# The first 26 MLP steps of a three-stage kernel, and all scan and weight work beside them, as static pinned lists

## The chip, the cores and the metric

One core of a Trainium2 chip runs the whole program. It has five engines with an instruction queue each, which run in order and wait for each other by semaphores: TensorE (PE, matmuls; PEld is its weight load), VectorE (DVE), ScalarE (ACT), GpSimd (POOL) and SyncE (SP, which issues most transfers here). The metric is the device time of one execution in microseconds. A kernel's time is the median of several runs; beside these stands one profiled execution, whose trace the rows below come from.

## The reference

A gated linear attention, an MLP with a silu gate and a top-1 mixture of eight experts, one after the other, all in 32-bit floats:

```python
f = 1.0 / (1.0 + np.exp(-f_logit))              # q, k, v, f_logit: (4, 8, 768, 48)
for t in range(S):
    state = f[:, :, t, :, None] * state + np.einsum('bhd,bhe->bhde', k[:, :, t], v[:, :, t])
    y[:, :, t] = np.einsum('bhd,bhde->bhe', q[:, :, t], state)
x = y.transpose(0, 2, 1, 3).reshape(3072, 384)
h = x @ w_in                                     # (384, 2048)
x = (h * (1.0 / (1.0 + np.exp(-h)))) @ w_out     # (2048, 384)
...
expert_idx = np.argmax(x @ w_gate, axis=1)       # 8 experts, 384 -> 1024 -> 384, relu
```

## The kernel before

The 3072 tokens are 24 chunks of 128 (six to a batch entry). A chunk n of the scan goes through these pieces of work: its gate logits f_n are clamped on DVE, go through exp and ln on ACT, and are summed along time by a matmul with a triangular matrix (pl_n); ACT makes en_n and ep_n of that; DVE multiplies them into k and q (kpad, qpad); PE transposes both (pk_n, pq_n), ACT copies them out (kt_n, qt_n); PE makes the scores (sc_n, two banks), DVE masks them (am_n); PE makes the outputs from the state, from the masked scores, and the gain of the state (py_n and pyb_n); ACT copies y_n, DVE carries the state, PE flips y_n (pt_n), and ACT and DVE make the high and low half of x from it (big for chunks 0 and 1, xth and xtl of group g after that). Chunks 0, 1 form group 0, chunks 2, 3 group 1, chunks 4 to 6 group 2, whose f is one tile, called f_4.

The MLP works on one group g and one sixteenth i of the 2048 hidden columns at a time; that pair is a step. `moe_h` makes ph_g_i (nine matmuls: high and low halves of x and w_in), then se (tanh, ACT) and sg (DVE); `moe_g` splits sg into gh (ACT) and gl (DVE); `moe_o`, two steps later, multiplies them by a piece of w_out into px (six matmuls for two chunks, nine for three). Steps 0 to 5 belong to group 0, steps 6 to 11 to group 1, and from step 12 on both take turns, hidden piece by hidden piece. In the same time 16 pieces each of w_in and w_out arrive, with 64 bits to a number; DVE converts a piece in three instructions (in_cv, out_cv), ACT takes the high half (in_hi, out_hi) and DVE the low one (in_lo, out_lo).

A long written list, `OPENING`, sets the order of everything ahead of step 0; its instructions are pinned, which means that they stay on their engine in the order in which they were written. Behind it a plan gives each piece of work a step (`ST0` to `ST6`, `UI`, `UO`, `LD`), and the loop over the steps writes a step's ph, its planned work, its split and its px. On PE that order is kept; on DVE, ACT and SP a scheduler orders the unpinned instructions at build time, by its own estimate of when they are ready. The PSUM banks of the tag a are three, and all of a chunk's pl, pk, pq, sc, py, pyb and pt take them in turn; a new tile waits until the readers of the tile before it in its bank are done.

Of the kernel before, what the change touches and what calls it, by code (L numbers as in the profile page):

```python
# [43 lines left out]
FILL = {2: 4}  # L44
# [3 lines left out]
ST0 = (-15, -12, -10, -8, -6, -4)  # L48
ST1 = (-12, -11, -7, -5, -3, -1)
ST2 = (-9, 0, 0, 1, 3, 4)  # L50
ST3 = (-1, 2, 3, 4, 5, 5)
ST4 = (-2, 3, 5, 7, 9, 11)
ST5 = (7, 10, 12, 16, 16, 18)
ST6 = (14, 17, 20, 22, 24, 26)
LAST = ((5, 4), (3, 5))
F_HOME = {2: 'lfh', 3: 'lfl'}
LD = (-30, -30, -10, -1, 0, 5, 11)
S1 = (-2, 1, 3, 5, 6, 8)
ASH = 3
# [7 lines left out]
UI = (-9, -9, -9, 0, 1, 1, 3, 5, 6, 8, 9, 11, 13, 15, 17, 19)  # L67
UO = (-9, -9, -9, 1, 2, 3, 5, 6, 8, 10, 11, 13, 15, 17, 19, 21)
# [4 lines left out]
GACT = 9  # L73
# [4 lines left out]
LOV = (0, 0)  # L78
# [7 lines left out]
ST = ST0, ST1, ST2, ST3, ST4, ST5, ST6  # L86
# [11 lines left out]
def kernel(  # L98
# [71 lines left out]
    BANKS = {0: "haahhaaa", 1: "haahhaaa"}  # L170
# [84 lines left out]
    def load_piece(kind, i):
        u, h = divmod(i, 4)
        src = moe_w_in if kind == "in" else moe_w_out
        nm = f"{kind}_{i}"
        if h == 0:
            new_unit((kind, u))  # L260
        shape = [P, KC, P] if kind == "in" else [P, 1, DM]
        if src.dtype == I64:
            t = raw.tile(shape + [2], U32, tag="raw", name=f"{nm}_raw")
            made = len(pieces_made)
            pieces_made.append(i)
            load_raw(t.rearrange("p c f w -> p c (f w)"), src, kind, i, nc.scalar if made < 0 else nc.sync)
            x = raw.tile([P, ROW], U32, tag="cv", name=f"{nm}_cv", bufs=2)[:, :DM].rearrange("p (c f) -> p c f", c=shape[1])
            t2 = t.rearrange("p c f w -> p (c f) w")
            narrow(t2, x.rearrange("p c f -> p (c f)"), i < (PI if kind == "in" else PO))
            x = x.bitcast(F32)  # L270
        else:
            x = raw.tile(shape, F32, tag="raw", name=f"{nm}_raw")
            nc.sync.dma_start(out=x, in_=part_of(src, kind, i, 1))
        split((kind, u), h, x if kind == "in" else x[:, 0], nc.vector)
# [58 lines left out]
    pieces_made = []  # L333
# [43 lines left out]
    def narrow(r, x, pin=False):  # L377
        for k in range(3):
            if pin and k == 0:
                strict.append(1)  # L380
            narrow_op(r, x, k, ve)
            if pin and k == 0:
                strict.pop()
# [9 lines left out]
    def clamp(t, pin=lambda fn: fn):  # L393
        pin(nc.vector.tensor_scalar_max)(t, t, FMIN)

    def log1(t, pin=lambda fn: fn):
        pin(nc.scalar.activation)(t, t, AF.Ln, bias=1.0)

    def att0(n):
        f = loaded.pop(("f", n))  # L400
        g, _ = group_of[n]
        if g < 2 or n == starts[g]:
            t = f if g < 2 else fb[g][:, : sizes[g]]
            pin = keep if g == 2 else lambda fn: fn
            if g != 2:
                clamp(t)
            pin(nc.scalar.activation)(t, t, AF.Exp, scale=-1.0)
            if g != 2:
                log1(t)
# [6 lines left out]
        (nc.scalar.copy if n < EARLY else nc.vector.tensor_copy)(hi, f2)  # L416
        nc.vector.tensor_sub(lo, f2, hi.bitcast(F32))
# [155 lines left out]
    def att4(n):  # L573
# [4 lines left out]
        warm(y_banks(n)[0], FILL.get(n, 0))  # L578
# [101 lines left out]
    def moe_h(g, i):  # L680
# [13 lines left out]
        (keep(nc.scalar.activation) if (g, i) == (0, 0) else nc.scalar.activation)(e, ph[:, :GT], AF.Tanh, scale=0.5)  # L694
        t = att.tile([P, GT], F32, tag="sg", name=f"sg_{g}_{i}", bufs=SG)
        nc.vector.scalar_tensor_tensor(out=t, in0=e, scalar=1.0, in1=ph[:, :GT], op0=ALU.add, op1=ALU.mult)  # L696
        ht[g, i] = t

    def moe_g(g, i):
# [4 lines left out]
        (nc.scalar.copy if g < GACT else nc.vector.tensor_copy)(hi, t)  # L704
        (nc.gpsimd if (g, i) < LOV else nc.vector).tensor_sub(lo, t, hi.bitcast(F32))  # L705
# [642 lines left out]
    for n in range(NCH):  # L1348
        g, r = group_of[n]
        if n < len(ST):  # L1350
            so = ST[n]
            s0 = ld = LD[n]
        else:
            s0 = pos[g, 0] - NF + r * NF // sizes[g] - ASH
            so = [s0 + x for x in S1]
            s0 = ld = s0 - 4
        if n == 2:
            at(so[1], spread_ends, 2, sy)
            at(so[1], lambda: (open_high("out", 2), open_low("out", 2)))
        for j, st in enumerate(stages):  # L1360
            if n > 1 and (n, j) not in OPENED:
                (at_end if (n, j) in LAST else at)(so[j], st, n)
        if g < 2:
            if n == 3:
                at(ld, load_chunk, n, "kq")
        else:
            if r == 0:
                for m in range(n, n + sizes[g]):
                    if g > 2:
                        at(s0, load_chunk, m, "f")  # L1370
            at(ld, load_chunk, n, "qk")
        if n > 2:
            at(ld + 1, load_chunk, n, "v")
    for i in range(16):
        for nm, slots in (("in", UI), ("out", UO)):
            if (nm, i) not in OPEN_PIECES:
# [184 lines left out]
```

## Time and profile before

| | |
|---|---|
| median of the runs (lowest to highest, 3 runs) | 837.82 us (836.27 to 840.59) |
| profiled execution: time, span | 833.39 us, 831.7 us |
| PE busy | 802.9 us, 97% of the span |
| DVE busy | 469.1 us, 56% |
| ACT busy | 377.4 us, 45% |
| POOL busy | 65.2 us, 8% |
| mean granted PE clock | 0.992 of full speed |
| transfers | 99.10 MB, mean 119 GB/s |

The span runs from the first instruction to the last. PE's busy time counts a matmul from start to modelled end, so it says when PE had work, not that the work went at full speed. Matmuls, and also the instructions of DVE and ACT, overlap a little with their followers; the cost of one in a dense stretch is read from start to start. Where an engine sat idle, the views name what ended the wait.

### The profile page before, as it was taken

What the parts mean: (1) busy time and instruction counts of PE and PEld (TensorE: products, weight loads), DVE (VectorE), ACT (ScalarE), POOL (GpSimd) and SP (SyncE); (2) the same over time, 40 slices, a digit from 0 to 9 for tenths busy, and PEclk for the clock granted to TensorE, in tenths of its full rate; (3) what the DMA queues carried; (4) which work ended last, traced back from release to release, by engine and by line L of the source; (5) the groups of instructions that cost most, each with busy time, mean ns of one, the idle gap of its engine ahead of it and who ended that gap; (6) DMA issues with size and microseconds to landing.
All of it is one profiled execution on the core that took longest, in us unless ns stands there. A gap on an engine that the chain in (4) does not pass through costs nothing.

```text
span 831.7 us, 15598 instructions
## 1 busy us (share of the span) xinstructions
PE 802.9 (97%) x5840; PEld 754.2 (91%) x5840; DVE 469.1 (56%) x1258; ACT 377.4 (45%) x836; POOL 65.2 (8%) x111
## 2 busy tenths in 40 slices
PE   8789989999999999999999999999999999999994
PEld 5679889989999999999999999999899999989994
DVE  7889964555555556646655646466574426245520
ACT  5644454453453454435445333355473426455520
POOL 2000100001000100100100000101200010111001
PEclk9999899999999999999999999999999999999998
DMA  9855546222443343342433321423281617645500
GB/s 215 205 153 159 182 127 202 65 51 67 110 93 86 96 105 79 105 104 65 119 81 77 95 82 40 134 58 125 90 291 44 206 39 265 221 145 169 170 16 28
DMA packets 171813, 99.10 MB, mean 119 GB/s; under 512 B 115756, under 2 KB 165341, under 8 KB 171728
## 3 DMA queue, kind: packets, MB, share of 16 engines
q1 hardware_dynamic: 167342, 87.34, 38.1%
q0 software_dynamic: 3280, 9.49, 3.1%
q10 hardware_dynamic: 1106, 1.18, 0.4%
q8 instruction: 48, 0.79, 0.4%
q14 instruction: 37, 0.30, 0.1%
HBM read 78.76 MB, written 16.33 MB: 114 GB/s over the span
## 4 chain that ended last, share of the span: by engine, by line
PE 77%; DVE 8%; issue 7%; DMA 3%; ACT 2%; POOL 1%; SPq 0%; POOLq 0%; ACTq 0%; DVEq 0%
PE ph L423 22%; PE px L423 22%; PE po L423 7%; PE p L423 7%; PE pya L423 3%; PE sc L423 3%; PE pyb L423 2%; PE pl L423 1%; PE pk L428 1%; PE plt L428 1%; DMA w_raw<-in_moe_w_dram 1%; POOL out_dram L1002 1%; PE p_r L423 1%; PE pq L428 1%; PE po_r L423 1%
## 5 line engine op out<-in xcount | busy, mean ns | idle before, releaser
L423 PE MATMUL px<-out_lo,gh 128*128 128x384 f32 x384 | 137.0, 357 | 0.3 <-ACT gh L704 0.3
L696 DVE SCALAR_TENSOR_TENSOR sg<-se,ph 128x384 f32<-128x384 f32 (+1 forms) x144 | 72.9, 507 | 113.1 <-ACT se L694 110.3
L694 ACT ACTIVATE se<-ph 128x384 f32<-128x384 f32 (+1 forms) x143 | 64.9, 454 | 150.2 <-PE ph L423 142.1
L423 PE MATMUL px<-out_hi,gl 128*128 128x384 f32 x384 | 129.5, 337 | 0.0
L423 PE MATMUL px<-out_hi,gh 128*128 128x384 f32 x384 | 128.8, 335 | 0.0
L423 PE MATMUL ph<-xth,in_lo 128*128 128x384 f32 (+1 forms) x384 | 124.3, 324 | 1.5 <-ACT xth L657 1.2
L423 PE MATMUL ph<-xtl,in_hi 128*128 128x384 f32 (+1 forms) x384 | 122.8, 326 | 2.5 <-DVE sg L696 1.9
L423 PE MATMUL ph<-xth,in_hi 128*128 128x384 f32 (+1 forms) x384 | 124.0, 323 | 0.0
L704 ACT CAST gh<-sg 128x384 fp32r<-128x384 f32 (+1 forms) x144 | 68.9, 478 | 63.3 <-DVE sg L696 60.6
L705 DVE TENSOR_TENSOR gl<-sg,gh 128x384 fp32r<-128x384 f32 (+1 forms) x144 | 73.5, 510 | 32.1 <-ACT gh L704 31.2
L423 PEld LDWEIGHTS ph<-xtl,in_hi 128*128 128x128 f32 x384 | 72.1, 189 | 4.3 <-DVE sg L696 2.6
L423 PEld LDWEIGHTS px<-out_lo,gh 128*128 128x128 f32 x384 | 72.3, 188 | 3.8 <-issue 1.1
L423 PEld LDWEIGHTS ph<-xth,in_lo 128*128 128x128 f32 x384 | 72.6, 189 | 2.4 <-ACT xth L657 1.4
L423 PEld LDWEIGHTS px<-out_hi,gl 128*128 128x128 f32 x384 | 72.3, 188 | 0.8 <-DVE gl L705 0.3
L423 PEld LDWEIGHTS ph<-xth,in_hi 128*128 128x128 f32 x384 | 72.6, 189 | 0.0
L423 PEld LDWEIGHTS px<-out_hi,gh 128*128 128x128 f32 x384 | 72.1, 188 | 0.0
L423 PE MATMUL po<-w_lo,hh 128*128 128x384 f32 (+4 forms) x184 | 62.9, 342 | 0.0
L423 PE MATMUL po<-w_hi,hl 128*128 128x384 f32 (+4 forms) x184 | 62.0, 337 | 0.0
L423 PE MATMUL po<-w_hi,hh 128*128 128x384 f32 (+4 forms) x184 | 61.9, 336 | 0.0
L253 DVE TENSOR_TENSOR w_lo<-w_raw,w_hi 128x384 fp32r<-128x384 f32 x104 | 52.5, 551 | 13.0 <-ACT w_hi L252 12.9
L423 PE MATMUL p<-xsl,w_hi 128*128 128x480 f32 (+6 forms) x168 | 58.4, 347 | 0.0
L423 PE MATMUL p<-xsh,w_hi 128*128 128x480 f32 (+6 forms) x168 | 58.3, 347 | 0.0
(290 smaller groups left out, 1465.4 us busy)
## 6 DMA issues: line engine op xcount, KB each, us to landing
w_raw<-in_moe_w_dram SPq DMA_DIRECT2D x64, 384.0 KB
xs<-big SPq DMA_DIRECT2D x8, 776.0 KB
in_again<-in_moe_w_in_dram SPq DMA_DIRECT2D x16, 384.0 KB
out_again<-in_moe_w_out_dram SPq DMA_DIRECT2D x16, 384.0 KB
in_raw<-in_moe_w_in_dram SPq DMA_DIRECT2D x15, 384.0 KB
xe<-xs SPq DMA_DIRECT2D x7, 776.0 KB
out_raw<-in_moe_w_out_dram SPq DMA_DIRECT2D x14, 384.0 KB
f<-in_f_logit_dram SPq DMA_DIRECT2D x24, 192.0 KB
```

Source lines behind the costliest of these rows:

```text
L253: (keep(lo_engine.tensor_sub) if pin else lo_engine.tensor_sub)(lo[:, h], x, hi[:, h].bitcast(F32))
L423: ins = nc.tensor.matmul(*a, **k)
L428: ins = nc.tensor.transpose(*a, **k)
L694: (keep(nc.scalar.activation) if (g, i) == (0, 0) else nc.scalar.activation)(e, ph[:, :GT], AF.Tanh, scale=0.5)
L696: nc.vector.scalar_tensor_tensor(out=t, in0=e, scalar=1.0, in1=ph[:, :GT], op0=ALU.add, op1=ALU.mult)
L704: (nc.scalar.copy if g < GACT else nc.vector.tensor_copy)(hi, t)
L705: (nc.gpsimd if (g, i) < LOV else nc.vector).tensor_sub(lo, t, hi.bitcast(F32))
L1002: ins = nc.gpsimd.indirect_dma_start(out=out[:, :], out_offset=bass.IndirectOffsetOnAxis(ap=idx[:n], axis=0), in_=o[:n], in_offset=None, b ...
```

## The change

Everything up to step 26 is now written out. `OPENING` ends a little differently, and a new list `STEPS` gives for each of the steps 0 to 26 three strings: what is written ahead of its ph, between ph and split, and behind its px. In these strings ci0:6 is the first conversion instruction of w_in piece 6, hi and Li its high and low half, co, ho, Lo the same for w_out, li and lo the loads; the other names are those of the scan's pieces of work. All of it is pinned, ph's tanh, sg, gh and gl too. A step converts one piece: two instructions ahead of ph, the third behind sg; the high and low half of a piece are made one step after its conversion. The gate logits of chunks 4 to 6 move from the opening to steps 1 to 4, with a table load on each side of their ln; those of chunks 7 to 9 are fixed in steps 17 to 21. The table that has tanh is loaded by hand behind ln of f_3. Chunk 1's sum takes another bank, the four warm-up matmuls ahead of chunk 2's outputs are dropped, and chunk 5 (the last of its batch entry) no longer writes its decay for the state.

```diff
-OPENING = '... kmul:1 qmul:1 ends:1 f:2 li:2 a:1 f:3 F:4 F:5 F:6 k:2 q:2 lo:2 sc:0 ...'
+OPENING = '... kmul:1 qmul:1 ends:1 f:2 f:3 li:2 a:1 k:2 q:2 li:3 sc:0 ... exp:2 log:2 exp:3 log:3 table:0 ...'
+STEPS = (
+    ('ci0:3 ci1:3', 'ci2:3 lo:3 fk:2 fq:2 kt:2 qt:2', ''),
...
+    ('co0:3 co1:3', 'co2:3 lo:6 hi:5 Li:5 st:2 fk:3 fq:3 kt:3 qt:3 a:3 fclamp:2 fexp:2', 'pt:2 xh:2 xl:2'),
...
-FILL = {2: 4}
...
-ST2 = (-9, 0, 0, 1, 3, 4)
-ST3 = (-1, 2, 3, 4, 5, 5)
-ST4 = (-2, 3, 5, 7, 9, 11)
...
-UI = (-9, -9, -9, 0, 1, 1, 3, 5, 6, 8, 9, 11, 13, 15, 17, 19)
-UO = (-9, -9, -9, 1, 2, 3, 5, 6, 8, 10, 11, 13, 15, 17, 19, 21)
...
-    BANKS = {0: "haahhaaa", 1: "haahhaaa"}
+    BANKS = {0: "haahhaaa", 1: "xaahhaaa"}
...
-        warm(y_banks(n)[0], FILL.get(n, 0))
...
-        (keep(nc.scalar.activation) if (g, i) == (0, 0) else nc.scalar.activation)(e, ph[:, :GT], AF.Tanh, scale=0.5)
+        ac.activation(e, ph[:, :GT], AF.Tanh, scale=0.5)
...
-        nc.vector.scalar_tensor_tensor(out=t, in0=e, scalar=1.0, in1=ph[:, :GT], op0=ALU.add, op1=ALU.mult)
+        ve.scalar_tensor_tensor(out=t, in0=e, scalar=1.0, in1=ph[:, :GT], op0=ALU.add, op1=ALU.mult)
...
+        table=lambda n: ac.preload_act_table_set("exp_and_others"),
...
-    for s in range(first, total):
-        if s >= 0:
-            moe_h(*seq[s])
+    for s in range(total):
+        pre, mid, end = STEPS[s] if s < len(STEPS) else ("", "", "")
+        if s == len(STEPS):
+            strict.clear()
+        steps(pre)
+        moe_h(*seq[s])
+        steps(mid)
         for fn, args in plan.get(s, ()):
             fn(*args)
-        if s >= 0:
-            moe_g(*seq[s])
+        moe_g(*seq[s])
         if s >= LAG:
             moe_o(*seq[s - LAG])
+        steps(end)
```

**Place 1: ACT ahead of step 0's tanh (se_0_0).** Before:

```order
L224 ACTIVATE f_3_237<-f_3_237 128x384 x2
L224 COPY y_1_365<-py_1_325 128x12x16
L224 COPY y_1_365<-pyb_1_326 128x12x16
L224 CAST in_0_hi_144<-in_2_cv_359 128x384
L224 CAST big_92<-pt_1_373 128x384
L224 ACTIVATE en_2_378<-pl_2_368 128x384
L224 ACTIVATE ep_2_380<-pl_2_368 128x384
L224 ACTIVATE f_4_239<-f_4_239 128x1152 x2
L224 ACT_TABLE_LOAD
L224 ACTIVATE se_0_0_415<-ph_0_0_402 128x256
```

and now:

```order
L236 ACTIVATE f_3_233<-f_3_233 128x384 x2
L236 ACT_TABLE_LOAD
L236 CAST big_92<-pt_0_339 128x384
L236 CAST in_0_hi_144<-in_1_cv_314 128x384
L236 COPY y_1_366<-py_1_329 128x12x16
L236 COPY y_1_366<-pyb_1_330 128x12x16
L236 CAST in_0_hi_144<-in_2_cv_363 128x384
L236 CAST big_92<-pt_1_374 128x384
L236 ACTIVATE en_2_379<-pl_2_369 128x384
L236 ACTIVATE ep_2_381<-pl_2_369 128x384
L236 ACTIVATE se_0_0_418<-ph_0_0_405 128x256
```

Both halves of f_3's work and the table load stand ahead of x high of chunk 0 (big from pt_0), and exp and ln of f_4 are gone from ahead of se_0_0.

**Place 2: PE at steps 2 and 3,** where chunk 2's outputs (py_2) and ph_0_3 follow px of step 0. Before:

```order
L423 MATMUL px_0_1_555<-out_0_hi_134,gh_0_0_451 128x384
L423 MATMUL ph_0_3_562<-big_92,in_0_hi_144 128x256
...
L423 MATMUL py_2_576<-ones_80 128x512
...
L423 MATMUL py_2_576<-state_86,qt_2_433 128x48
...
L423 MATMUL py_2_576<-v_2_392,am_2_0_479 128x48
...
L423 MATMUL py_2_576<-v_2_392,kpad0_89 64x48 x8
L428 MATMUL pq_3_611<-ident_77,qpad1_88 112x128 x4
L428 MATMUL pk_3_616<-ident_77,kpad1_90 112x128 x4
```

and now:

```order
L408 MATMUL px_0_1_537<-out_0_hi_134,gh_0_0_439 128x384
L408 MATMUL py_2_544<-state_86,qt_2_437 128x48
...
L408 MATMUL py_2_544<-v_2_297,am_2_0_483 128x48
...
L408 MATMUL py_2_544<-v_2_297,kpad0_89 64x48 x8
L408 MATMUL ph_0_3_578<-big_92,in_0_hi_144 128x256
...
L413 MATMUL pk_3_599<-ident_77,kpad1_90 112x128 x4
L413 MATMUL pq_3_604<-ident_77,qpad1_88 112x128 x4
```

The outputs of chunk 2 stand ahead of ph_0_3, without the matmuls on ones, and k is transposed ahead of q. Chunk 3's outputs move ahead of ph_0_5 in the same way; those of chunks 4 to 6 move by one to three steps, in either direction.

**Place 3: DVE from the carry of chunk 2 to the masks of chunk 3.** Before:

```order
L595 TENSOR_TENSOR state_86<-py_2_576,state_86 112x4x48
L596 TENSOR_TENSOR state_86<-state_86,a_all_85 112x4x48
L452 SCALAR_TENSOR_TENSOR kpad0_89<-en_4_627,k_4_441 128x8x48
L458 TENSOR_TENSOR qpad0_87<-q_4_439,ep_4_629 128x8x48
L224 TENSOR_SCALAR out_5_cv_638<-out_5_raw_636 128x384
L369 SCALAR_TENSOR_TENSOR out_5_cv_638<-out_5_raw_636,out_5_cv_638 128x384
L696 SCALAR_TENSOR_TENSOR sg_0_4_674<-se_0_4_672,ph_0_4_662 128x256
L373 SCALAR_TENSOR_TENSOR out_5_cv_638<-out_5_raw_636,out_5_cv_638 128x384
L661 TENSOR_TENSOR xtl_1_681<-pt_2_676,xth_1_680 128x384
L705 TENSOR_TENSOR gl_0_4_699<-sg_0_4_674,gh_0_4_698 128x256
L523 TENSOR_TENSOR am_3_0_694<-sc_3_0_684,trir_78 128x512
L253 TENSOR_TENSOR out_1_lo_541<-out_5_cv_638,out_1_hi_540 128x384
```

and now:

```order
L236 TENSOR_TENSOR state_86<-py_2_544,state_86 112x4x48
L236 TENSOR_TENSOR state_86<-state_86,a_all_85 112x4x48
L236 TENSOR_SCALAR f_4_491<-f_4_491 128x1152
L236 TENSOR_TENSOR gl_0_3_618<-sg_0_3_590,gh_0_3_617 128x256
L236 TENSOR_TENSOR xtl_1_632<-pt_2_627,xth_1_631 128x384
L236 TENSOR_SCALAR out_4_cv_635<-out_4_raw_463 128x384
L236 SCALAR_TENSOR_TENSOR out_4_cv_635<-out_4_raw_463,out_4_cv_635 128x384
L236 SCALAR_TENSOR_TENSOR sg_0_4_650<-se_0_4_648,ph_0_4_638 128x256
L236 SCALAR_TENSOR_TENSOR out_4_cv_635<-out_4_raw_463,out_4_cv_635 128x384
L236 TENSOR_TENSOR out_0_lo_135<-out_3_cv_575,out_0_hi_134 128x384
L236 TENSOR_TENSOR am_3_0_667<-sc_3_0_657,trir_78 128x512
L236 TENSOR_TENSOR am_3_1_669<-sc_3_1_658,trir_78 128x512
```

The clamp of f_4 stood in the opening and is now here, ahead of gl_0_3; conversions come one piece to a step where they came two pieces side by side. On ACT the same stretch now reads:

```order
L236 COPY kt_3_609<-pk_3_599 112x512
L236 COPY qt_3_611<-pq_3_604 112x512
L236 ACTIVATE f_4_491<-f_4_491 128x1152
L236 CAST gh_0_3_617<-sg_0_3_590 128x256
L236 CAST xth_1_631<-pt_2_627 128x384
L236 ACTIVATE se_0_4_648<-ph_0_4_638 128x256
L236 CAST out_0_hi_134<-out_3_cv_575 128x384
L236 CAST gh_0_4_671<-sg_0_4_650 128x256
L236 ACT_TABLE_LOAD
L236 ACTIVATE f_4_491<-f_4_491 128x1152
L236 ACT_TABLE_LOAD
L236 COPY y_3_709<-py_3_683 128x12x16
```

Here exp of f_4 stands ahead of gh_0_3, and its ln with two table loads ahead of the copy of y_3; before, both stood in the opening (place 1).

## Rows read from the trace of the kernel before

**Rows 1.** Windows view, a row per stretch: its length, busy PE, PEld, DVE, ACT, POOL, PEclk

```profile
24.70:61.50 36.80, 29.08 (x256) 25.14 (x256) 30.42 (x70) 20.02 (x43) 0.00 (x0) 1.00 0.70 185
61.50:92.00 30.50, 30.15 (x248) 28.83 (x248) 28.65 (x71) 15.35 (x39) 0.00 (x0) 1.00 0.52 150
92.00:102.00 10.00, 9.07 (x48) 8.10 (x48) 9.66 (x23) 3.92 (x11) 3.19 (x1) 0.66 0.59 193
102.00:119.00 17.00, 14.72 (x107) 13.24 (x107) 9.58 (x24) 10.95 (x21) 1.87 (x2) 1.00 0.70 190
119.00:142.00 23.00, 23.00 (x177) 22.89 (x178) 12.34 (x30) 9.39 (x25) 0.88 (x5) 1.00 0.45 151
```

**Rows 2.** Waits of PE from 24.7 to 142 us: in total, times, longest

```profile
PE ph L423 <- DVE sg L696: 1.9, 2, 1.5
PE sc L423 <- ACT kt L500: 1.4, 1, 1.4
PE pk L428 <- ACT y L570: 1.4, 1, 1.4
PE ph L423 <- DVE in_lo L253: 1.3, 1, 1.3
...
PE ph L423 <- ACT in_hi L224: 1.1, 1, 1.1
...
PE py L423 <- DVE am L523: 0.7, 1, 0.7
```

**Rows 3.** Windows view around 95 us, columns as in rows 1

```profile
94.00:95.00 1.00, 1.00 (x13) 0.91 (x11) 1.00 (x4) 0.00 (x0) 0.82 (x1) 0.73 0.93 311
95.00:101.00 6.00, 6.00 (x26) 5.71 (x27) 5.75 (x14) 1.94 (x6) 2.37 (x1) 0.50 0.54 174
101.00:102.00 1.00, 1.00 (x5) 0.85 (x4) 0.91 (x3) 1.00 (x4) 0.00 (x0) 0.86 0.94 304
```

**Rows 4.** Timeline of PE: start, us, instruction, count, around chunk 2's outputs

```profile
38.30 1.04 PE L423 MATMUL py<-ones 128*128 128x512 bf16 x4
39.27 0.31 PE L423 MATMUL py<-state,qt 48*128 48x48 f32 x1
...
42.81 0.65 PE L428 MATMUL pq<-ident,qpad 128*112 128x128 f32 x4
```

**Rows 5.** Timeline of DVE near 90 us: start, us, instruction

```profile
89.21 0.41 DVE L696 SCALAR_TENSOR_TENSOR sg<-se,ph 128x256 f32<-128x256 f32 x1
89.54 0.35 DVE L365 TENSOR_SCALAR out_cv<-out_raw 128x384 uint32<-128x384 uint32 x1
89.81 0.55 DVE L369 SCALAR_TENSOR_TENSOR in_cv<-in_raw,in_cv 128x384 uint32<-128x384 uint32 x1
90.28 0.55 DVE L369 SCALAR_TENSOR_TENSOR out_cv<-out_raw,out_cv 128x384 uint32<-128x384 uint32 x1
...
92.36 1.28 DVE L523 TENSOR_TENSOR am<-sc,trir 128x512 f32<-128x512 f32 x2
93.55 0.54 DVE L253 TENSOR_TENSOR in_lo<-in_cv,in_hi 128x384 fp32r<-128x384 f32 x1
```

**Rows 6.** Timeline of ACT ahead of step 0's tanh

```profile
25.28 2.38 ACT L224 ACTIVATE f<-f 128x1152 f32<-128x1152 f32 x2
27.67 1.28 ACT L224 ACT_TABLE_LOAD   x1
28.96 0.38 ACT L224 ACTIVATE se<-ph 128x256 f32<-128x256 f32 x1
```

**Rows 7.** Timeline of DVE: the one conversion that waited for its piece

```profile
103.37 0.36 DVE L365 TENSOR_SCALAR in_cv<-in_raw 128x384 uint32<-128x384 uint32 x1 [0.85 <-DMA in_raw<-in_moe_w_in_dram]
```

**Rows 8.** Chain that ended last: start, us, groups of matmuls

```profile
46.38 1.05 PE px L423 x6
47.42 1.06 PE ph L423 x9
48.81 1.09 PE sc L423 x16
```

More of the change, by code (lines that the diff above doesn't have):

```diff
@@ L77 @@
 PD = 2
-LOV = (0, 0)
 VS = 44
@@ L250, in split @@
         pin = key[0] in ("w1", "w2") and key[1] == 0 or key[:2] == ("w1", 1)
-        pin_hi = pin or (key, h) == (("in", 0), 3)
-        (keep(nc.scalar.copy) if pin_hi else nc.scalar.copy)(hi[:, h], x)
+        (keep(nc.scalar.copy) if pin else nc.scalar.copy)(hi[:, h], x)
         (keep(lo_engine.tensor_sub) if pin else lo_engine.tensor_sub)(lo[:, h], x, hi[:, h].bitcast(F32))
[L255 to L274, printed above, removed]
     opened = {}
@@ L375, in narrow_op, with narrow @@
             )
-    def narrow(r, x, pin=False):
+    def narrow(r, x):
         for k in range(3):
[L379 to L383, printed above, removed]
+            narrow_op(r, x, k, nc.vector)
     lf = {}
@@ L401, in att0 @@
         g, _ = group_of[n]
[L402 to L409, printed above, removed]
+        if g > 3 and n == starts[g]:
+            for k in range(3):
+                f_group(g, k)
         if n < PLAIN:
@@ L1047, in rest_fetch @@
         w = nt * P
-        r = [raw.tile([P, ROW], F32, tag="cv", name=f"xe_r_{t}", bufs=2) for t in range(nt)]
+        r = [raw.tile([P, ROW], F32, tag="cv", name=f"xe_r_{t}", bufs=CVB) for t in range(nt)]
         for t in range(nt):
@@ L1349 @@
         g, r = group_of[n]
[L1350 to L1359, printed above, removed]
-        for j, st in enumerate(stages):
[L1361 to L1376, printed above, removed]
-                at(slots[i], load_piece, nm, i)
+        if n < LISTED:
+            continue
+        s0 = pos[g, 0] - NF + r * NF // sizes[g] - ASH
+        for j, st in enumerate(stages):
+            at(s0 + S1[j], st, n)
+        s0 -= 4
+        if g > 3 and r == 0:
+            for m in range(n, n + sizes[g]):
+                at(s0, load_chunk, m, "f")
+        at(s0, load_chunk, n, "qk")
+        at(s0 + 1, load_chunk, n, "v")
     for j in range(2 * NF):
@@ new lines, with steps @@
+    for nm, kind in (("i", "in"), ("o", "out")):
+        do["l" + nm] = lambda i, kind=kind: open_load(kind, i, queue((kind, i) in FIRST))
+        do["h" + nm] = lambda i, kind=kind: open_high(kind, i)
+        do["L" + nm] = lambda i, kind=kind: open_low(kind, i)
+        do["c" + nm] = lambda i, kind=kind: [open_join(kind, i, k) for k in range(3)]
+        for part in range(3):
+            do[f"c{nm}{part}"] = lambda i, kind=kind, part=part: open_join(kind, i, part)
+    def steps(text):
+        for step in text.split():
```

105 lines of the change are left out of this document (39 added, 66 removed), and 25 rows, old and new, of the table STEPS.

## The prediction

> **What bounds the kernel now.** I first took the windows view, to see in which stretch TensorE (PE) leaves time unused [rows 1]. From 119 us on, PE is busy without a gap, and the pages of the stretches behind show the same dense picture; what can be won lies between 24.7 us, where MLP step 0 starts, and 119 us. The reader is to take the length less the PE busy time of each row: 36.80 - 29.08 = 7.72, 30.50 - 30.15 = 0.35, 10.00 - 9.07 = 0.93 and 17.00 - 14.72 = 2.28, together 11.28 us idle.
>
> The waits of PE say what those gaps are [rows 2]: single waits, most of them 1.1 to 1.5 us long, each for another engine's result: the gated product sg on VectorE (DVE), the transposed keys on ScalarE (ACT), the y copy that frees a PSUM bank, the low and the high half of a weight piece, the masks. None is a long lack of data; they are results that an in-order engine made too late because other work stood ahead of them. In the first window DVE is busy for 30.42 of 36.80 us, in the second for 28.65 of 30.50: DVE is nearly full while it converts the weight pieces, and it works far ahead: after 119 us it is busy for only 12.34 of 23.00.
>
> The windows around 95 us show a second loss [rows 3]: the granted clock goes from 1.00 to 0.50 (1.2 in place of 2.4 GHz) for about seven microseconds. Lost are 0.27 + 6 x 0.50 + 0.14 = 3.41 us of PE at full clock. Just before, chunk 5's 48-column products had waited for their masks (am, 0.7 in [rows 2]).
>
> Last, the four warm-up matmuls ahead of chunk 2's output take from 38.30 to 39.27 us [rows 4]: 0.97 us of PE on nothing. **The most the change can give** is thus 11.28 + 3.41 + 0.97 = 15.7 us.
>
> **The change, part by part.** It leaves the amount of work as it is (but for the four warm-ups, two more table loads and three small transfers for chunk 5, whose state nobody reads) and fixes who stands behind whom on every engine up to step 26. I cost it by what still waits afterwards.
>
> The DVE load first. Start to start, DVE takes 0.33 for sg, 0.27 for the first conversion instruction, 0.47 for each of the other two and for a low half, 1.19 for a pair of masks [rows 5]. A piece is 0.27 + 3 x 0.47 = 1.68, a step with its sg and gl 1.68 + 2 x 0.33 = 2.34. A PE step is one ph and one px: 1.06 + 1.05 = 2.11 [rows 8]. So in steps without attention work DVE is the slower by 0.23; the attention matmuls turn it round: a chunk costs PE some 6 us (two transpose groups of 0.65 and outputs from 39.27 to 42.81, 3.54 [rows 4], scores 1.09 [rows 8]) and DVE an estimated 3.2, by the nearest forms of [rows 5] (k and q products and x low like a low half, 3 x 0.47, masks 1.19, two narrow state operations 0.6). Over 26 steps and nearly five chunks PE has 26 x 2.11 + 4.9 x 6 = 84 us and DVE 27 x 1.68 + 26 x 0.66 + 4.9 x 3.2 = 78, plus 2 for clamps and splits of f. PE stays the longer one, and before sg each new step has two conversion instructions that fill the time in which DVE would wait for ph and its tanh. A PE step needs gl of two steps earlier, so a lag of some 4 us on DVE costs nothing. I cost the steady part of the list at nothing; the cover is that lag. If it went, each of some 14 steps without much attention would lose 0.23, 3.2 us.
>
> *Step 0.* Before, ACT has behind ep of chunk 2 the exp and ln of chunks 4 to 6 (2.38) and a table load (1.28), and only then tanh of step 0, at 28.96 [rows 6]. These 3.66 us leave this place. In exchange exp and ln of f_3 and the table load now stand ahead of x high of chunk 0: 1.28 and an estimated 0.8 (a third of the 2.38, for a third of the columns), while before ACT had to wait there for the flip of y; DVE gives some of it back, because the clamp of f_4 to f_6 (an estimated 0.7, three times the columns of an instruction of 0.27) has left the opening. I expect step 0 to start within 0.5 us of before and the scores of chunk 2 about 1.6 us earlier. The waits for kt (1.4), for the weight halves of piece 3 (1.1 and 1.3) and for the y copy (1.4) go, since piece 3 is converted in step 0 and needed in step 3, and chunk 2's outputs stand a step earlier. Left here: about 0.4 for q's product and 0.6 for the masks of chunk 2, together 1.0.
>
> *Step 4, where a new wait comes.* The clamp of f_4 now stands on DVE behind the state of chunk 2; behind it stands gl_0_3, which needs gh_0_3, and gh_0_3 stands on ACT behind exp of f_4, which needs the clamp. So DVE waits for exp (1.19, half of the pair in [rows 6]) and gh (0.4, as long as sg): 1.6. From the end of ph_0_3, DVE needs 0.4 (tanh, [rows 6]) + 0.33 + 0.47 + 0.47 + 0.6 + 0.7 = 3.0 to the end of the clamp, then 1.6 + 0.33 (gl) + 0.47 (x low) + 0.27 + 0.47 + 0.33 + 0.47 + 0.47 to the masks of chunk 3 and 0.6 for the first: 5.0, together 8.0. PE has in that time two transpose groups, px, the flip of y, ph_0_4, the scores and px: 1.3 + 1.05 + 0.35 (half a transpose group) + 1.06 + 1.09 + 1.05 = 5.9; the outputs of chunk 3 then need a bank that the first mask frees, so PE waits for about 2.1 us. I take 2.5, since each hand-over between engines adds a little. Bounds: 0 if the wait for exp is met by slack, and 4 if exp of f_4 finds its data late as well (a wait as long as the longest in [rows 2] on top).
>
> *Table loads.* The ln of f_4 and of f_7 each stand between two loads: 1.28 + 1.19 + 1.28 = 3.75 us of ACT. At step 4 this lies beside chunk 3's outputs (3.5 us of PE), whose copy is next on ACT; it costs next to nothing. At step 21 it lies beside chunk 6's outputs, but f_7's split waits on DVE for ln, about 2.4 us of DVE in steps without attention; what of it reaches PE I put at 1.1. Bounds 0 and 2.4. In the row, tanh starts at 28.96, 0.01 us after the load's 28.95: a load costs 1.28 here. The Trainium skill, page "ScalarE: Activation LUTs", section "What ACT_TABLE_LOAD costs", counts a drain of about 1.38 us on top of the load, 2.66 in all; by that the two loads at step 4 would block ACT for 2.8 us more, the y copy and the next tanh would come that much later, and the gain would be an estimated 2.8 us smaller. The row shows no such drain, so the sum goes by the row.
>
> *Transfers.* SyncE's list now has f_4 to f_6 behind weight piece 5, which takes three transfers out of the opening, and every piece is asked for about four steps ahead of its conversion, some 13 us, where the buffer of the piece four back is free by then. The v loads wait in the same queue for the chunk before; the pieces behind them still have over 10 us. Before, one conversion waited 0.85 us for its piece [rows 7]. I take 0; bounds 0 and 0.85 for each of a few pieces, 2 us.
>
> **Sum.** New waits: 1.0 + 2.5 + 1.1 = 4.6. Gain 15.7 - 4.6 = 11.1, if the clock stays up. Against the profiled execution (span 831.7, 833.39 in all) that is 822.3. The runs shown have a median of 837.82, 4.4 above that execution; I take the same gain from it: **826.7, said as 827**. Steps from 27 on keep their order on PE, and PE was full there, so the shift carries to the end.
>
> **Rivals.**
> *The clock falls again (0.27).* Between 94 and 95 us it fell after waits of under 1 us among chunk 5's narrow products [rows 2, 3], while waits of 1.1 to 1.4 around chunk 2, with the four warm-ups there, brought none. The wait before chunk 3's outputs, 2.5 us, stands among the same products and has no warm-ups. Price 3.4: gain 7.7, 830. The Trainium skill, page "TensorE: Matmul & The Clock Gate", section "Why this matters for your kernels", wants idle gaps of PE kept short and lets only long ones drop the clock; by that the clock would never have fallen in this trace, where no wait between steps 0 and 26 is over 1.5 us, and it would not fall at step 4 either, which is the forecast's 827. The trace disagrees, so I leave the fall a chance.
>
> *DVE becomes the bound (0.15).* If hand-overs eat the lag, PE waits in nearly every step: 0.23 in 14 steps is 3.2. With the upper bounds of step 4 and of the transfers (1.5 and 2) the gain is about 4: 834, inside what counts as no change. For it: DVE at 28.65 of 30.50. Against: the same row has PE at 30.15.
>
> *Late pieces behind a fixed order (0.05), the slower side.* Every step now opens on DVE with two conversions; if its piece has not landed, sg, gl and all of attention stand behind it, where the order of before had other work. Twenty-seven pieces are converted from step 0 on. The gain is gone, and half a percent (4.2 us) lost on top, when each is (11.1 + 4.2) / 27 = 0.57 us late. At the 0.85 of [rows 7] for each, 23 us: 850. Against it: the DMA share from 24.7 us on is 0.70, 0.52, 0.59, 0.70, not full.
>
> **How the numbers follow.** Forecast 0.53, own range 824 to 829 from the bounds of step 4 (0 to 4) and of the second table pair. Clock 0.27, 828 to 832. DVE bound 0.15, 831 to 836. Late pieces 0.05. A range of **822.5 to 834** leaves out the late pieces, the upper part of the third case and a little on the low side: 0.15 to 0.2. Half a percent, 4.2 us, is about what a measurement of this kernel tells from no change: the forecast and the clock case lie beyond it (0.80), the third case straddles it (0.02 faster, 0.13 same), and the late pieces are slower beyond it; with 0.01 moved there for what I have not thought of: faster 0.81, same 0.13, slower 0.06.
>
> **What will show it.** Tanh of step 0 right behind ep of chunk 2, and no wait of PE for kt, in_hi, in_lo or the y copy between steps 0 and 4; chunk 2's outputs done some 6 us earlier; one wait of about 2.5 us before chunk 3's outputs, named by the masks; the granted clock at 1.00 around steps 14 to 16. Group 1's first ph some 7 us earlier; step 26 some 11 earlier. Wrong would be: conversions that wait for DMA, a clock of 0.50 near chunk 3, or waits of PE for gl in most steps of 12 to 25.

## The result, and the profile after

The changed kernel took 829.06 us (median of 4 runs, 828.56 to 829.73) against 837.66 of the kernel before in the same comparison: a ratio of 0.9893, 95% interval 0.9866 to 0.9921. Its profiled execution took 829.73 us, with a span of 827.6 and a mean granted clock of 0.984.

The windows view of the changed kernel, in the stretches of [rows 1]:

```profile
24.70:61.50 36.80, 34.67 (x254) 31.93 (x255) 26.51 (x61) 19.14 (x41) 0.00 (x0) 0.81 0.55 136
61.50:92.00 30.50, 29.67 (x257) 27.93 (x255) 28.15 (x69) 14.15 (x36) 0.00 (x0) 1.00 0.56 151
92.00:102.00 10.00, 9.84 (x72) 9.33 (x72) 7.88 (x19) 6.15 (x16) 0.00 (x0) 1.00 0.56 149
102.00:119.00 17.00, 14.85 (x124) 14.28 (x124) 13.11 (x32) 10.76 (x21) 0.75 (x4) 0.98 0.93 261
119.00:142.00 23.00, 23.00 (x153) 22.96 (x152) 17.27 (x46) 10.34 (x27) 1.44 (x5) 0.94 0.54 183
```

PE's idle time is 2.13 + 0.83 + 0.16 + 2.15 = 5.27 us where it was 11.28. The granted clock is the other way round: 1.00 in four of the five rows before, now below 1.00 in three of five. Its falls in finer windows, each window with its clock third from the end:

```profile
36.00:37.00 1.00, 1.00 (x10) 0.91 (x11) 0.96 (x3) 0.00 (x0) 0.00 (x0) 0.63 1.04 228
37.00:43.00 6.00, 6.00 (x38) 5.91 (x38) 4.06 (x11) 2.49 (x6) 0.00 (x0) 0.50 0.97 215
43.00:44.00 1.00, 1.00 (x9) 0.97 (x8) 0.33 (x1) 0.63 (x1) 0.00 (x0) 0.96 0.86 304
49.00:50.00 1.00, 1.00 (x14) 0.94 (x12) 0.96 (x4) 0.99 (x2) 0.00 (x0) 0.95 0.91 299
50.00:56.00 6.00, 6.00 (x40) 5.82 (x40) 0.31 (x1) 1.73 (x3) 0.00 (x0) 0.50 0.17 39
56.00:57.00 1.00, 1.00 (x7) 1.00 (x6) 0.32 (x1) 0.73 (x3) 0.00 (x0) 0.63 0.20 40
118.00:119.00 1.00, 1.00 (x6) 1.00 (x5) 1.00 (x4) 1.00 (x4) 0.00 (x0) 0.59 1.00 333
119.00:121.00 2.00, 2.00 (x11) 2.00 (x10) 1.97 (x6) 0.74 (x3) 0.00 (x0) 0.50 1.06 278
121.00:122.00 1.00, 1.00 (x6) 1.00 (x5) 1.00 (x3) 0.64 (x2) 0.20 (x1) 0.71 0.20 39
```

A window at clock c spent 2 (1 - c) of its length at half speed: 0.74 + 6 + 0.08 = 6.8 us in the first fall, 0.1 + 6 + 0.74 = 6.8 in the second, 0.82 + 2 + 0.58 = 3.4 in the third. That is 17.0 us at half speed, 8.5 of PE work by the reckoning of the prediction, against 3.41 in [rows 3].

The waits of PE, as in [rows 2]:

```profile
PE pt L413 <- ACT y L236: 2.2, 1, 2.2
PE pyb L408 <- DVE am L236: 1.2, 2, 1.0
PE pq L413 <- DVE xtl L236: 1.0, 2, 0.8
PE ph L408 <- ACT big L236: 0.8, 1, 0.8
PE py L408 <- DVE am L236: 0.7, 1, 0.7
PE pq L413 <- DVE qpad L236: 0.3, 1, 0.3
```

The waits for kt, for the halves of piece 3, for sg and for the y copy ahead of pk are gone. The place where the stage ends can be read from the first gate sum of chunk 7, in a step that PE reaches in the same order in both kernels; before:

```profile
137.69 0.33 PE L423 MATMUL pl<-lfh,trir 128*128 128x384 f32 x1
```

and now:

```profile
133.68 0.33 PE L408 MATMUL pl<-lfh,trir 128*128 128x384 f32 x1
```

4.0 us earlier. From there to the end of the span it is 694.0 us before and 693.9 now: nothing is lost or won behind the stage. The 4.0 are more than the reckoning gives: 6.0 less of idle time and 0.97 of warm-ups, less 5.1 for the falls, would be 1.9. The falls may have cost less than half of their length; the experiments come back to this.

**Two executions are not two medians.** The spans of the two profiles differ by 4.1 us, the medians by 8.6. With the experiments below, the kernel before ran 65 times. Its mean granted clock lies from 0.975 to 0.992, median 0.986, and its time rises by 0.65 us for each 0.001 of clock less (a straight line through the 65 pairs, correlation -0.91). Its profiled execution, at 0.992, was as high as any of them. The line gives 837.2 us at a clock of 0.985; the line through the ten runs of the changed kernel gives 829.2. At the same clock the change is worth 8.0 us, and the clock itself is on average 0.985 before and 0.984 now. These means have in them a fall at the end of the span, where PE has nothing left to do: 6.8 us long in the profile before, 9.7 and 9.1 in the changed kernel's two. It costs no time but moves the mean by up to 0.002, so the 8.0 us is good to about 1 us.

### The profile page after: what moved, and what is told of

It reads as the page before. It is cut to its first block, busy times and chain, and to the rows that moved or that the text cites. A ratio compares the mean times of both kernels' runs of the same rounds, so it can differ in the third digit from the quotient of the medians.

```text
span 827.6 us, 15612 instructions
## 1 busy us (share of the span) xinstructions
PE 804.3 (97%) x5836; PEld 758.3 (92%) x5836; DVE 468.6 (57%) x1258; ACT 378.0 (46%) x838; POOL 61.3 (7%) x111
## 5 line engine op out<-in xcount | busy, mean ns | idle before, releaser
L677 DVE SCALAR_TENSOR_TENSOR sg<-se,ph 128x384 f32<-128x384 f32 (+1 forms) x117 | 61.8, 528 | 109.7 <-ACT se L675 108.1
L675 ACT ACTIVATE se<-ph 128x384 f32<-128x384 f32 (+1 forms) x117 | 55.0, 470 | 141.1 <-PE ph L408 135.4
L685 ACT CAST gh<-sg 128x384 fp32r<-128x384 f32 (+1 forms) x117 | 57.9, 495 | 51.7 <-DVE sg L677 49.4
L686 DVE TENSOR_TENSOR gl<-sg,gh 128x384 fp32r<-128x384 f32 (+1 forms) x117 | 62.2, 532 | 28.5 <-ACT gh L685 27.1
```

Of the source, the lines that this page charges most:

```text
L675: ac.activation(e, ph[:, :GT], AF.Tanh, scale=0.5)
L677: ve.scalar_tensor_tensor(out=t, in0=e, scalar=1.0, in1=ph[:, :GT], op0=ALU.add, op1=ALU.mult)
L685: ac.copy(hi, t)
L686: ve.tensor_sub(lo, t, hi.bitcast(F32))
```

## The experiments

Each edit is to the changed kernel unless it says otherwise. Ratios are to the kernel before in the same comparison.

| run | median us | runs | ratio, 95% interval | median clock |
|---|---|---|---|---|
| changed kernel again | 830.37 | 6 | 0.9926 (0.9898 to 0.9954) | 0.984 |
| four warm-ups back | 829.65 | 9 | 0.9912 (0.9881 to 0.9943) | 0.986 |
| before, no warm-ups | 836.08 | 12 | 0.9988 (0.9963 to 1.0013) | 0.979 |
| exp of f behind gh | 828.51 | 12 | 0.9920 (0.9891 to 0.9948) | 0.988 |
| exp of f_4 behind xth | 829.02 | 6 | 0.9897 (0.9863 to 0.9931) | 0.985 |
| y_6 ahead of ln f_7 | 830.62 | 10 | 0.9949 (0.9915 to 0.9983) | 0.985 |
| f_4 back in the opening | 830.26 | 9 | 0.9928 (0.9902 to 0.9954) | 0.985 |
| three moves | 825.51 | 6 | 0.9854 (0.9817 to 0.9892) | 0.991 |
| no pins from step 0 on | 843.24 | 6 | 1.0084 (1.0057 to 1.0111) | 0.974 |
| no pins on DVE | 823.32 | 6 | 0.9832 (0.9794 to 0.9870) | 0.987 |
| halves in the same step | 850.69 | 6 | 1.0164 (1.0124 to 1.0205) | 0.978 |
| the same, no pins on DVE | 821.40 | 6 | 0.9817 (0.9763 to 0.9871) | 0.992 |

**The same kernel again.**

> The changed kernel once more, nothing edited, for a second profile and as a comparison on this chip. Theory A (the falls of the granted clock sit where PE waits among narrow products): the fall at chunk 3's outputs is there again, others may come and go; median within 1 us of 829.06. Span times mean granted clock (the length that the same work would have at full clock) near 815, as in its first runs, against near 823 for the kernel before; the mean clock near 0.985 for both.

The fall at chunk 3's outputs was there again, from 48.5 to 55.3 us, and the one behind the flip of y_6; the one at chunk 2 was not, though nothing had been edited. The wait before chunk 3's outputs is now as long as the prediction had it, since PE came to it at full clock:

```profile
PE pyb L408 <- DVE am L236: 2.5, 2, 2.3
PE pt L413 <- ACT y L236: 2.2, 1, 2.2
```

**Warm-ups.**

```diff
+        fill=lambda n: warm(y_banks(n)[0], 4),
-    (..., 'past:2 own:2 pu:2 y:2 v:3'),
+    (..., 'fill:2 past:2 own:2 pu:2 y:2 v:3'),
```

> The changed kernel with one thing put back: four matmuls on ones ahead of chunk 2's outputs. Theory A (the dropped warm-ups cost a fall of the granted clock, which in the changed kernel's profile lasts from 36.6 to 43.0 us): PEclk stays at 1.00 from 30 to 46 us, PE gains about 3.1 us of clock and pays 0.97 for the four, so some 2 us less than the changed kernel's 829.06, near 827. Rival B (the warm-ups have nothing to do with the clock; the narrow products fall anyway): the fall is still there, a little later, and the time is 0.5 to 1 us above 829.06, near 830. Falls two and three (50 to 57 and 118.6 to 121.6 us) are left alone by both.

and in the kernel before:

```diff
-FILL = {2: 4}
+FILL = {}
```

> The kernel before without the four matmuls on ones ahead of chunk 2's outputs, nothing else. Theory A (they kept the clock up there): a fall to 0.50 follows chunk 2's waits near 40 us, 3.1 us lost for 0.97 saved, some 2 us above the kernel before. Rival B: no fall near 40 us, and 0.5 to 1 us below the kernel before.

With the four put back there was no fall near 36 us, but its profile shows one of 10.2 us that ends at 28.6, ahead of them, and the median is where it was. Without them the kernel before fell from 43 to 50 us, as theory A had it, and in four more places by 109 us; its clock is 0.979 in the median where 0.986 was usual. Its time did not rise. PE's idle time from 24.5 us to the sum of chunk 7, added up over half-microsecond windows, is 5.75 us in this profile against 11.27. Among the waits that are gone are those of 1.4 for the y copy, 1.2 for xth and 1.5 for sg, whose places now lie in a fall or behind one; it fits that DVE and ACT catch up while PE runs at half speed. So a fall costs less than half of its length where PE would wait for other engines anyway, and theory A's price, not its mechanism, was wrong. The clock is lower without the warm-ups, and the time can't be told from the same (ratio 0.9963 to 1.0013): what they keep of the clock and the 0.97 us that they take are about even.

**The wait before chunk 3's outputs.** These rows of the changed kernel, of DVE and then of ACT, show what holds the masks back:

```profile
42.58 0.75 DVE L236 TENSOR_SCALAR f<-f 128x1152 f32<-128x1152 f32 x1
44.86 0.42 DVE L236 TENSOR_TENSOR gl<-sg,gh 128x256 fp32r<-128x256 f32 x1 [1.53 <-ACT gh L236]
...
47.84 1.28 DVE L236 TENSOR_TENSOR am<-sc,trir 128x512 f32<-128x512 f32 x2
```

```profile
43.37 1.17 ACT L236 ACTIVATE f<-f 128x1152 f32<-128x1152 f32 x1 [0.91 <-DVE f L236]
44.44 0.39 ACT L236 CAST gh<-sg 128x256 fp32r<-128x256 f32 x1
...
47.44 1.28 ACT L236 ACT_TABLE_LOAD   x1
48.74 1.17 ACT L236 ACTIVATE f<-f 128x1152 f32<-128x1152 f32 x1
49.91 1.28 ACT L236 ACT_TABLE_LOAD   x1
```

DVE's gl waits 1.53 us for gh, gh stands behind exp, exp waits for the clamp: the chain of the prediction. Two runs took it apart. The first has these two edits:

```diff
-    ('co0:3 co1:3', '... a:3 fclamp:2 fexp:2', 'pt:2 xh:2 xl:2'),
+    ('co0:3 co1:3', '... a:3 fclamp:2', 'fexp:2 pt:2 xh:2 xl:2'),
-    ('ci0:13 ci1:13', '... fclamp:3 fexp:3', ''),
+    ('ci0:13 ci1:13', '... fclamp:3', 'fexp:3'),
```

> The changed kernel with exp of the gate logits f_4 (and f_7) written behind the high half gh of the same step in place of ahead of it. Both theories: DVE's wait of 1.53 us for gh (and that of 1.52 at f_7) goes, the masks of chunk 3 end about 1.5 us earlier, and PE's wait of 0.99 for them goes. Theory A (a fall needs a wait of PE together with narrow products): the fall from 50 to 57 us goes too, 1.0 + 3.1 us less, near 825. Rival B (the 48-column products are enough): the fall stays, and the time is 1.0 less, near 828.

The wait only moved: x low now waited 1.26 us for xth, which stood behind exp, and PE waited 2.1 for the masks. The second run has exp of f_4 behind xth (`'pt:2 xh:2 fexp:2 xl:2'`) and leaves exp of f_7 where it was:

> The changed kernel with exp of f_4 written behind the high half of chunk 2's x (xth) in place of ahead of gh of step 3; DVE's clamp stays. Theory A: neither gl nor x low waits for exp any more, the masks of chunk 3 end some 1.4 us earlier, PE's wait for them (2.1 to 2.3 us where the clock was up just before) is under 1 us, and the clock falls less often at chunk 3's outputs; span times clock 1.4 less than the changed kernel's, time 1.4 to 3 us less. Rival B: DVE's conversions are the limit there and the wait stays at 2 us, time unchanged.

Its waits of PE, and its windows at chunk 3's outputs (52.05 to 56.2 us) and behind the flip of y_6:

```profile
PE pt L413 <- ACT y L236: 2.2, 1, 2.2
PE pq L413 <- DVE xtl L236: 1.0, 2, 0.8
PE py L408 <- DVE am L236: 0.7, 1, 0.7
PE pyb L408 <- DVE am L236: 0.2, 1, 0.2
```

```profile
48.00:58.00 10.00, 9.86 (x100) 9.04 (x98) 6.12 (x15) 7.51 (x13) 0.00 (x0) 1.00 0.32 90
117.00:119.00 2.00, 0.70 (x5) 0.71 (x6) 1.17 (x4) 1.91 (x5) 0.00 (x0) 1.00 1.08 314
119.00:123.00 4.00, 4.00 (x19) 4.00 (x18) 3.97 (x10) 2.36 (x7) 0.20 (x1) 0.57 0.72 225
```

The wait is 0.2 and the clock stays at 1.00 through the outputs. Yet this execution fell at 20 and at 40 us instead, and the medians don't separate it from the changed kernel. The profile shows both sides: from the first matmul of step 0 to the first gate sum of chunk 7 it takes 106.5 us (28.44 to 134.97), where the changed kernel's two profiles take 110.7 and 109.4, but step 0 starts 5 us later, behind the fall at 20 us, in an opening that the edit doesn't touch. Part of what the stage gains may be owed to that fall, in which the other engines get ahead: PE's wait of 0.8 us for x high is gone too. Over all runs, span times clock is 815.2 us on average against 814.5 for the changed kernel, where theory A had it 1.4 lower. So it isn't shown that the time falls by the wait that went.

**f_4 back in the opening** (its loads, clamp, exp, ln and the table load; nothing of it in steps 1 to 4).

> The changed kernel with one move undone: loads, clamp, exp and ln of f_4 to f_6 and the tanh table back in the opening, ahead of step 0. By the steps of the prediction: tanh of step 0 later by the 2.4 + 1.3 us of ACT that stand ahead of it again, less what the opening's earlier load gave back, chunk 2's scores some 2 us later, and in exchange no wait of PE before chunk 3's outputs (2.1 to 2.3 us). Theory A: the two cancel, within 1.5 us of the changed kernel. Rival B (the late start of step 0 is absorbed by slack ahead of chunk 2): 2 us less than the changed kernel.

The wait before chunk 3 is 0.2 here too, and the clock does not fall there; in exchange PE waits 2.2 us for x high at step 0, with a fall 1.1 us behind that wait, and 0.6 for qt. The two cancel, as theory A had it.

**The flip of y_6, and three moves together.**

```diff
-    ('co0:13 co1:13', '...', 'flog:3 table:0 own:6 pu:6 y:6'),
+    ('co0:13 co1:13', '...', 'own:6 pu:6 y:6 flog:3 table:0'),
```

> The changed kernel with ACT's copy of y_6 written ahead of the two table loads and ln of f_7. Theory A (the 2.15 us that PE waits to flip y_6 come from this pair of loads alone, and the third fall comes from that wait): the wait is under 0.3 us, PEclk is 1.00 around 119 us, 2.0 + 1.6 us less, near 825.5. Rival B (the split of f_7 on DVE, which waits for ln and then holds sg, is late next): PE waits about as long for sg or gl in the steps behind, and the time stays within 1 us of 829.

The 2.2 us for y_6 went, and PE waited 1.5 us for sg instead: rival B, to that extent. DVE showed why: the split of f_7 (lfh), whose unpinned instructions the scheduler had put into step 22 ahead of sg, waited 1.25 us for ln. No fall followed. The next kernel keeps this move, has exp of f_4 behind xth and pins the split behind step 26:

```diff
-        ve.tensor_copy(hi, f2)
-        ve.tensor_sub(lo, f2, hi.bitcast(F32))
+        first = keep if n == PLAIN else lambda fn: fn
+        first(nc.vector.tensor_copy)(hi, f2)
+        first(nc.vector.tensor_sub)(lo, f2, hi.bitcast(F32))
```

> The changed kernel with three moves: exp of f_4 behind xth of chunk 2, ACT's copy of y_6 ahead of the loads and ln of f_7, and DVE's split of f_7 pinned behind step 26 in place of step 22, where it waited 1.41 us for ln and held sg. Theory A (falls of the clock follow PE's waits): the waits before chunk 3's outputs (2.2) and before the flip of y_6 (2.15) go, no wait of over 1 us is left between steps 3 and 26, and the falls that followed these two are gone; those in the opening and at chunk 2 stay. 4.3 us of waits and one or two falls of 1.3 to 2.6: 822 to 825. Rival B (other waits and other falls take their place): 828 or more.

825.5 us, a little over the range of theory A. After the one fall at chunk 2 the clock stays up:

```profile
36.00:43.00 7.00, 7.00 (x44) 6.82 (x44) 4.72 (x12) 2.51 (x7) 0.00 (x0) 0.51 0.95 212
43.00:142.00 99.00, 95.81 (x755) 89.55 (x755) 78.90 (x195) 53.76 (x123) 2.43 (x9) 1.00 0.59 171
```

One wait over 1 us was left, against theory A: 1.5 for sg, whose tanh stands behind the two loads and ln on ACT.

**Falls and waits, over the twelve profiles of the changed kernel and its variants.** Where PE waited about 1 us or more (0.98 to 2.98) before or among chunk 3's outputs (the changed kernel twice, warm-ups back, exp behind gh, y_6 first, halves in the same step, and the three kernels without pins on DVE), the clock fell during those outputs, 9 times of 9; where that wait was 0.2 (three kernels), 0 of 3. Behind a wait of 2.15 us or more for the flip of y_6 it fell 6 times of 6; where that wait was under 1 us or absent, 0 of 6. Two more waits of that length were followed by a fall: 2.2 us for x high with f_4 in the opening, and 2.9 for qt with the halves in the same step. Single waits of 1.2 to 1.5 us between the wide matmuls of ph and px (y_6 first, three moves, no pins) brought no fall, and neither did 1.9 and 1.5 ahead of pq with the halves in the same step.

Other places keep this from being a rule. During chunk 2's outputs the clock fell in 8 of the 12, seven times behind a wait of 0.65 to 1.5 us and once behind none; the changed kernel itself, with a wait of 0.65 both times, fell there once and once not. During chunk 4's outputs it fell in 3 of the 12 (warm-ups back, exp behind gh, halves in the same step without pins on DVE), and PE has no wait between 62 and 82 us in these. So runs of 48-column products are sometimes enough without a wait, which is what rival B of exp behind gh said; that the waits make a fall more likely is what the counts show, and how they do it is not. Chunk 5's outputs, where [rows 3] has its fall, saw none in any of the twelve, while the kernel before fell there in both of its profiles, behind waits of 0.75 and, without warm-ups, 0.74 us. Falls ahead of step 0 came and went with no edit near them.

**The pins.** From step 0 on, no engine but PE keeps its written order:

```diff
     total = NG * NF
+    strict.clear()
```

> The changed kernel with the pins taken off from step 0 on: the same lists in the same steps, PE's order the same, but DVE, ACT and SP ordered by the scheduler as before. Theory L (the gain is in which step each piece of work stands, and in PE's order): within 2 us of the changed kernel. Rival P (the gain is in the fixed order on DVE and ACT): half or more of the 8.6 us is lost, 833 or more.

843.2, but not for either reason alone: the hand-written table load and f_4's work moved into the opening, and ACT loaded tables 14 times in the first 142 us in place of 6 (24 in place of 16 in all, so 8 loads were added, and not the 13 that the next expectation names). It says what an unpinned table load does, and nothing on DVE. So DVE alone:

```diff
-            return keep(fn) if strict else fn
+            return keep(fn) if strict and not (loose and self.eng is nc.vector) else fn
     total = NG * NF
+    loose.append(1)
```

> The changed kernel with the pins taken off DVE alone from step 0 on; ACT, SP and PE keep their written order, so that no table load moves (the earlier run without any pins brought 13 table loads more and says nothing on the rest). Theory L (which step each piece stands in and PE's and ACT's order carry the gain): within 2 us of the changed kernel's 829. Rival P (DVE's fixed order carries it: the scheduler puts conversions of later pieces ahead of sg again): DVE's waits for sg and gl reach PE as in the kernel before, 833 or more.

823.3 us: neither theory. The fixed order on DVE does not carry the gain, it costs about 6 us of it: the slowest of the six runs, 825.0, is faster than the fastest of the changed kernel's ten, 827.7. The 20 us between this kernel and the one without any pins belong to the pins on ACT and SP, which were not taken off one by one. PE's waits of 0.2 us and more from 20 to 142 us are one row, and the windows from 61.5 us on are full:

```profile
PE pyb L409 <- DVE am L506: 1.1, 1, 1.1
```

```profile
61.50:92.00 30.50, 30.50 (x266) 29.01 (x265) 28.44 (x69) 14.46 (x38) 0.00 (x0) 1.00 0.58 162
92.00:102.00 10.00, 10.00 (x82) 9.60 (x81) 8.55 (x22) 6.34 (x17) 0.00 (x0) 1.00 0.59 148
102.00:119.00 17.00, 17.00 (x137) 16.77 (x136) 15.95 (x40) 12.19 (x25) 1.04 (x4) 1.00 0.86 243
```

**The halves, one step behind or not.** Every `hi`, `Li`, `ho`, `Lo` written right behind the conversion of its piece:

```diff
-    ('ci0:6 ci1:6', 'ci2:6 li:8 ho:5 Lo:5 pl:4 ...', ''),
-    ('co0:6 co1:6', 'co2:6 lo:8 hi:6 Li:6', ''),
+    ('ci0:6 ci1:6', 'ci2:6 hi:6 Li:6 li:8 pl:4 ...', ''),
+    ('co0:6 co1:6', 'co2:6 ho:6 Lo:6 lo:8', ''),
```

> The changed kernel with the high and low half of a piece made in the step of its conversion, right behind it, in place of one step later. Theory S (the step between them is what keeps the in-order DVE from waiting for ACT's high half): each low half waits about 0.5 us, the length of ACT's cast, behind its conversion; 0.5 x 24 pieces is 12 us of DVE in steps where DVE's 2.34 us stand against PE's 2.11, so PE loses 4 to 12 us, 833 to 841. Rival (the lag of two steps between split and px absorbs it): within 1 us of 829.

850.7, more than theory S's upper end. DVE's waits, 13 and 10 of 0.58 us:

```profile
DVE out_lo L236 <- ACT out_hi L236: 7.5, 13, 0.6
...
DVE in_lo L236 <- ACT in_hi L236: 5.8, 10, 0.6
```

That is 13.3 us on DVE, and PE is idle for 19.6 us in the stretches of [rows 1]. With DVE unpinned as well:

> The halves in the step of their conversion, as in the run that took 850.7 us, and DVE without pins from step 0 on, as in the run that took 823.3 us. Theory U (the step between conversion and halves is needed only because DVE's order is fixed; a scheduler puts other work between ACT's high half and DVE's low one): the 23 waits of 0.58 us of DVE for the high halves are mostly gone, PE's idle time between 24.7 and 142 us is under 5 us, and the time is 823 to 828. Rival V (the written order itself makes ACT's high halves late for everybody): most of the 21 us stay, 838 or more.

821.4, a little below the range of theory U, with its mechanism: the waits of DVE for the high halves are gone, PE is idle for 2.8 us. The two kernels without pins on DVE can't be told apart, and the medians of both are below the changed kernel's; two of the six runs here took 828.3 and 828.5, at a clock of 0.983 and 0.987.

No run puts single places of the lists back, the earlier outputs of chunk 2 or the one piece to a step, say. Which of them carry the 8 us is not shown; the warm-ups, f_4's place and DVE's fixed order don't.

## Why the prediction came out as it did

The time lies in the range, 2 us above the forecast, and the direction is right. The forecast's own case, a clock that stays up (824 to 829), is not what happened; the rival whose clock falls (828 to 832) is. A clock of 0.50 near chunk 3, which the prediction named as a sign of being wrong, was there in both profiles of the changed kernel. Group 1's first ph came 1.6 us earlier in the first profile and 2.6 in the second (59.33 before, then 57.75 and 56.73), where 7 was said, and the sum of chunk 7 in step 26 came 4.0 and 4.7 earlier, where 11 was said.

- **The sum without the clock** is 11.28 + 0.97 - 4.6 = 7.65 us; at equal clock the runs show 8.0. That they agree so well is in part luck, since the waits were sized too low: from 24.5 us to the sum of chunk 7, PE idles for 7.5 us in the second profile, not 4.6. About 0.6 us of the difference comes back in PE's busy time, since the first matmul behind a wait takes 0.23 us to the next where 0.12 is usual and there are five waits fewer, 8 in place of 13; the rest is not accounted for.
- **Opening and masks:** tanh of step 0 starts at 25.95, not long behind ep of chunk 2, where it started at 28.96 [rows 6], and the scores of chunk 2 at 28.29, 2.1 us earlier (said: 1.6). Left are 0.8 for x high, 0.3 for q's product and 0.8 for masks, 1.9 in all (said: 1.0).
- **Step 4:** 2.3 us where PE came at full clock (said: 2.5), by the chain named, as exp behind xth shows (0.2 left); 0.99 in the first profile, where PE had gone through a fall just before.
- **Table loads:** the pair at step 4 cost nothing. The pair at step 21 cost 2.15 (said: 1.1), and not by the split of f_7 alone: the copy of y_6 stood behind it, which the prediction saw for y_3 and not here. In the rows above, ln starts at 48.74 behind a load that ends at 48.72: the drain of about 1.38 us that the Trainium skill ("ScalarE: Activation LUTs", "What ACT_TABLE_LOAD costs") adds to a load is not seen here either.
- **Transfers:** no wait of DVE for a transfer between 24 and 142 us; the 0 was right, and late pieces did not occur.
- **DVE at nothing:** the steady part of the list was put at nothing, with the lag as cover. Wrong by about 6 us, which the comparison with the kernel before does not show; only DVE without pins does. The lag covered the steps without attention, as said (0.83 and 0.16 us idle from 61.5 to 102). Which of the pinned places costs the 6 us was not taken apart; the waits for chunk 3's masks, x low of chunk 4 (0.8) and the flip of y_6 (2.2) are shorter or gone without the pins, and two of the three falls in the first profile stood behind such waits.
- **The step that failed is the clock term, 3.41 us.** The sum took the fall at chunk 5 as won back and put the changed kernel's own falls at nothing. The fall at chunk 5 did go, but others came, at the outputs of chunks 2 and 3 and behind the flip of y_6: 17.0 us at half clock in the first profile, 10.2 behind step 0 in the second. Over many executions both kernels have nearly the same clock, 0.985 and 0.984, which is sure to about 0.002. The assumption that the median would gain what the profile gains had the same root: that profile was among the least disturbed executions, and the 4.4 us between it and the median were mostly clock, 0.992 against 0.986, which is 3.9 us by the line. The waits of 1 us among narrow products that were followed by a fall side with [rows 3]. The Trainium skill ("TensorE: Matmul & The Clock Gate", "Why this matters for your kernels") lets only long idle gaps drop the clock. By that the falls behind waits of 0.65 to 1.0 us would not have come, nor those at chunk 4 behind none, and the runs disagree. The longest waits, 4.4 us for y_6 with the halves in the same step and 3.9 in the kernel without pins, had a fall too, as by the Trainium skill they would.

## What to carry to other kernels

Before a fall of the clock in one profile is booked as a loss that a change can win back, its share in other executions of the same kernel has to be known; the list of clocks per run gives it. And it has to be asked where the next fall will come. Here a written order on ACT and SP kept hand-placed table loads where they belonged; on DVE, which was nearly full, the written order cost more than the stalls it removed. On such an engine every producer on another engine needs a step of distance, which a free order found by itself. A wait in which two engines hold each other up went when the instruction that nobody near waited for, exp, was moved behind both that others waited for; moved behind one of them, it only held up the next. What that is worth in time showed only together with other moves (825.5 us).

## What the runs showed of the hardware that was not expected

All falls of the granted clock up to 180 us in these profiles lasted close to 3.4, 6.8, 10.2 or 20.5 us, and PE went at half clock in them: the matmuls of px with 384 columns, 0.17 us apart at full clock, were 0.32 apart. Where PE had no wait, a fall cost nearly half of its length: chunk 3's outputs and the ph behind them took 7.75 us in the changed kernel's second profile, with a fall of 6.8 in them, and 4.71 at full clock with exp behind xth, which is 0.45 us for each us of fall. Over whole runs the price was lower: 0.65 us for 0.001 of mean clock, which is 1.67 us at half speed in 835, so 0.39 us for each. That waits which would have come anyway are hidden in a fall fits this; it was seen in the kernel before without its warm-ups, and in the changed kernel, whose wait before chunk 3's outputs is 0.99 us where a fall went before and 2.31 where none did. What starts the falls ahead of step 0 stays open.
